# One gate of six with both products in one PSUM bank, on a fused Fourier-mixing and gated-MLP kernel

## The chip, the cores and the metric

The kernel runs on one core of one Trainium2 chip. Five engines work side by side, each through its own instructions in order: TensorE (PE in the profile; its weight loads are PEld), VectorE (DVE), ScalarE (ACT), GpSimd (POOL) and SyncE (SP), which only issues DMA transfers here. The metric is the device time of one execution in microseconds. Before the change three executions took 630.81, 631.33 and 631.26 us, median 631.26 us.

## The reference: what is computed

Input x is 8 batches of 3008 tokens with 256 channels. Both Fourier transforms, over tokens and over channels, are kept as their real part, and the result goes token by token through a gated MLP of width 1536:

```
X = np.fft.fft(x, axis=1)
X = np.fft.fft(X, axis=2)
x = X.real.reshape(8 * 3008, 256)
gate = np.maximum(x @ w_gate, 0.0)
val  = x @ w_val
out  = (gate * val) @ w_out
```

The kernel takes and gives float32; matmuls run on bfloat16 operands.

## The kernel before, in words

**The mirror trick.** The real part of a two-dimensional transform of real data is a sum of a cosine part and a sine part, and the token at the mirrored position has the same cosine part and the sine part with the other sign. So the kernel transforms half the tokens of a batch into two tiles: `U` (cosine, 128 channels by 1505 token columns) and `V` (sine). The channel transform is folded into the weights once: `WA[0]`, `WB[0]` are the gate's weights behind the cosine and sine part, `WA[1]`, `WB[1]` the value's, and `WM = -2 WB` with row 0 zero. A token has gate `a + s` and its mirror `a - s`, with `a = WA·U` and `s = WB·V`.

**Channel 128** has no row of its own among the 128 partitions. Its weights are row 0 of `WB`, and row 0 of `V` carries its values. `b2` holds the gate's channel-128 weights turned upright, one column for each of the 12 groups of 128 hidden units, and `CB` (called `c` in a tile's record) holds channel 128's values on all partitions.

**Tiling.** A batch b ≥ 1 has three blocks of token columns (512, 512 and 481: `thirds`), each with 12 tiles `fi` of 128 hidden units: 36 tiles per batch, 252 in all. Batch 0 has four blocks of 376 or 377 columns (`segments`) and an older form of tile (`first_tile`, `single_tile`).

**A tile of batches 1 to 7** passes through four functions in three successive slots:
- `seed` (L1010): ScalarE writes `c · b2` into a PSUM bank `p`. There are two `p` banks, so it waits until the tile two before has been read out of the same bank.
- `sine_part` (L1015, L1018): TensorE makes `-2s` in bank `g`; ScalarE copies it to a tile `q`. There is one `g` bank.
- `cosine_part` (L1022): TensorE adds `a` into the seeded bank `p`.
- `both` (L1026, L1027): VectorE makes `sp = p - q/2 = a + s`, which frees the bank `p`; GpSimd makes `sm = sp + q = a - s`.
- `value` (L874, L875): TensorE makes the value `a + s` in one of two banks `v`; `relu_mult` (L910) on VectorE multiplies it with `max(sp, 0)`. In the next slot `mirror` (L880) turns the bank `v` into `a - s`, and `second` (L910 again) multiplies it with `max(sm, 0)`.

**A slot** is written out by hand, and nothing reorders it. `slot(cur, mid, nxt, after)` handles four consecutive tiles: `sine_part` of `nxt`; five eighths of the slot's output matmuls (L781, which multiply finished hidden tiles `h` with `wo`); `cosine_part` of `nxt`; `seed` of `after`; `mirror` and `second` of the tile before `cur` (`pending`); `value` and `relu_mult` of `cur`; `both` of `nxt`; one eviction of an output bank on ScalarE, if one is due (L794); the rest of the output matmuls. So the tile `nxt` in the slot of tile `fi` is `fi + 2`. After some slots come three matmuls of the next batch's token transform (`DFT_EVEN`, `DFT_1`: after slots 0, 2, 6 and 8 of the first two blocks), with an eviction (L592, L595) and VectorE sums (L597) behind them. GpSimd folds the input of later batches in between (L198 to L222).

**One exception**: tile 6 of batch 1's first block (`kind` "o") takes the older form, with three matmuls into `g` (`gate`, then `mirror`) and two ScalarE evictions (L890).

**Start of batch 1.** The last tile of batch 0 also starts tiles 0 and 1 of batch 1 (`last`), and the `lead` slot, that of tile 0, follows. In batch 0 every group of output matmuls is followed by `flush`, which issues all due evictions. `gate_128` (L833 to L837) makes `b2` in batch 0's third block with twelve matmuls of one column and a VectorE copy. The weights' own matmuls (`weights`, L427 to L433) are spread over the tiles of batch 0's first block.

Of the kernel before, what the change touches and what calls it, by code (L numbers as in the profile page):

```python
# [29 lines left out]
def dram(ap, offset, pattern):  # L30
    return bass.AP(ap.tensor, offset, [list(p) for p in pattern])
# [3 lines left out]
def kernel(  # L35
# [8 lines left out]
    nc = tc.nc  # L44
    B, S, D = x.shape
    DF = moe_w_gate.shape[1]
    NF = DF // 128
# [3 lines left out]
    NK = NE + NJ  # L51
# [234 lines left out]
    kvec = single("kvec", [128, NK])  # L286
# [133 lines left out]
    def weights(c):  # L420

        f = slice(c * 512, (c + 1) * 512)

        def one(i, T, W):
            p = psO.tile([128, 512], F32, name="o", tag="o")
            for kc in range(2):
                nc.tensor.matmul(p[:], lhsT=T[:, kc, :], rhs=wr[i][c][:, kc, :], start=(kc == 0), stop=(kc == 1))  # L427
            if (i, c, W) == (0, 1, WA):
                return lambda: nc.scalar.copy(W[i][:, f], p[:])
            if (i, W) in ((1, WA), (c - 1, WB)):  # L430
                nc.vector.tensor_scalar(W[i][:, f], p[:], scalar1=1.0, op0=ALU.mult, scalar2=None)  # L431
# [25 lines left out]
    for t in range(3):  # L457
        n = ROWS[1][t]
# [46 lines left out]
    b2 = single("b2", [128, NF])  # L505
    one = single("one", [1, 1], BF16)
    nc.vector.memset(one[:], 1.0)


    def even_table(n, c):  # L510
# [311 lines left out]
    fold_even()  # L822
    turns_and_rows()

    more = {(0, i): [s] for i, s in enumerate(weights(1) + weights(2))}
    for n, c in enumerate(even_order):
        for k, step in enumerate(even_table(n, c)):
            more.setdefault(divmod(EVEN_AT[n] + k, NF), []).append(step)
# [1 line left out]
    for seg in (2, 3):  # L830
        more.setdefault((1, 8 + seg), []).append(lambda seg=seg: minus_v(nc.scalar, seg))

    def gate_128():  # L833
        p = psD.tile([128, 512], F32, name="d", tag="d")
        for f in range(NF):
            nc.tensor.matmul(p[:, f:f + 1], lhsT=WB[0][0:1, f * 128:(f + 1) * 128], rhs=one[:], start=True, stop=True)
        nc.vector.tensor_scalar(b2[:], p[:, 0:NF], scalar1=1.0, op0=ALU.mult, scalar2=None)  # L837
    more[(2, 2)] = [gate_128]
    more_1 = {}
    for at, step in zip((-5, -4, -3, -2, -1, 7, 7, 8, 14, 17), channel_loads() + channel_turn()):  # L840
        (more_1 if at >= 0 else more).setdefault(at if at >= 0 else (3, NF + at), []).append(step)

# [34 lines left out]
    def mirror(bank, st, i):  # L877

        W, v = (WB, st["vm"]) if st["b"] == 0 else (WM, st["vs"])
        nc.tensor.matmul(bank[:, 0:st["n"]], lhsT=W[i][:, st["f"]], rhs=v, start=False, stop=True, skip_group_check=True)  # L880

    def bank(tag):
        return {"g": psG, "p": psP, "v": psV, "d": psD}[tag].tile([128, 512], F32, name=tag, tag=tag)

    def space():
        return rp.tile([128, 512], F32, name="r", tag="r", bufs=12)

    def relu(st):
        st["r"] = space()
        nc.scalar.activation(st["r"][:, 0:st["n"]], st["g"][:, 0:st["n"]], ACTF.Relu)  # L890

    def half_h(st, sign):

        n = st["n"]
        return st["h"][:, 2 * n - 1:n - 1:-1] if sign else st["h"][:, 0:n]

    def mult(st, sign, r=None):
        n = st["n"]
        nc.vector.tensor_tensor(half_h(st, sign), (r or st["r"])[:, 0:n], st["v"][:, 0:n], op=ALU.mult)  # L899

    def keep_rest(st):
        o, h0 = 2 * REST * (st["b"] - 1) % 256, 896
        while h0 < 962:
            k = min(962 - h0, 256 - o)
            nc.sync.dma_start(out=LB[:, st["fi"], o:o + k], in_=st["h"][:, h0:h0 + k])
            o, h0 = 0, h0 + k

    def relu_mult(st, sign):
        n = st["n"]
        nc.vector.scalar_tensor_tensor(half_h(st, sign), in0=st["s"][1 + sign][:, 0:n], scalar=0.0, in1=st["v"][:, 0:n],  # L910
                                       op0=ALU.max, op1=ALU.mult)
# [28 lines left out]
    def single_tile(st, outs, extra=(), last=(), tag="p"):  # L940

        gate(st, tag)
        if pending is not None:
            finish(pending)
        value(st)
        mult(st, 0)
        run(todo_out, outs)
        for step in extra:
            step()
        mirror(st["g"], st, 0)  # L950
        relu(st)
# [52 lines left out]

    def seed(st, p=None):

        if st is None or st["kind"] == "o":
            return
        st["p"] = p or bank("p")
        nc.scalar.activation(st["p"][:, 0:st["n"]], st["c"], ACTF.Copy, scale=b2[:, st["fi"]:st["fi"] + 1])  # L1010

    def sine_part(st):
        n = st["n"]
        st["g"] = bank("g")
        nc.tensor.matmul(st["g"][:, 0:n], lhsT=WM[0][:, st["f"]], rhs=st["vs"], start=True, stop=True)  # L1015
        q = space()
        st["s"] = q, space(), q
        nc.scalar.copy(q[:, 0:n], st["g"][:, 0:n])  # L1018

    def cosine_part(st):  # L1020
        n = st["n"]
        nc.tensor.matmul(st["p"][:, 0:n], lhsT=WA[0][:, st["f"]], rhs=st["us"], start=False, stop=True, skip_group_check=True)  # L1022

    def both(st):
        n, (q, sp, sm) = st["n"], st["s"]
        nc.vector.scalar_tensor_tensor(sp[:, 0:n], in0=q[:, 0:n], scalar=-0.5, in1=st["p"][:, 0:n], op0=ALU.mult, op1=ALU.add)  # L1026
        nc.gpsimd.tensor_tensor(sm[:, 0:n], sp[:, 0:n], q[:, 0:n], op=ALU.add)  # L1027

    def slot(cur, mid, nxt, after, outs, fold_us):
# [5 lines left out]
        old = nxt is not None and nxt["kind"] == "o"  # L1035
        new = nxt is not None and not old
        if old:
            gate(nxt)
        lead = cur["lead"]
        if lead:  # L1040
            out(5)
        if new and mid["kind"] != "o":
            sine_part(nxt)
        out(3 if not lead else 5)
        out(5)
        if new and mid["kind"] == "o":
            sine_part(nxt)
        if new:
            cosine_part(nxt)
        seed(after)  # L1050
        if pending is not None:
            mirror(pending["v"], pending, 1)
        if pending is not None:
            second(pending)
        value(cur)
        if cur["kind"] == "o":
            mult(cur, 0, cur["first"])
        else:
            relu_mult(cur, 0)
        if new:  # L1060
            both(nxt)
        if old:
            nxt["first"] = nxt["r"]
            mirror(nxt["g"], nxt, 0)
            relu(nxt)
        run_fold(fold_us)
        run_one(evict)
        run_one(sums)
        out(8)
        return cur  # L1070
# [142 lines left out]
```

## Time and profile before

| what | value |
|---|---|
| median of three executions | 631.26 us |
| the profiled execution's own time | 630.98 us |
| its span, first to last instruction | 629.2 us |
| PE busy | 620.5 us (99%) |
| DVE busy | 551.5 us (88%) |
| POOL busy | 502.7 us (80%) |
| ACT busy | 445.5 us (71%) |
| granted TensorE clock | 1.00 |

A matmul's row in the timeline gives its start and its length; rows overlap, because matmuls are pipelined, so the step from one start to the next is what a matmul takes of TensorE's time. A row `x5` is five instructions in a run, with the length of the whole run. The brackets at the end of a row give the idle time of its engine just before it, and what ended that. In the groups of instructions the columns are count, busy time, mean length in ns, idle time before them and its releasers.

### The profile page before, as it was taken

The page shows a single profiled execution, that of the slowest core. Times are in us where ns is not written, and L with a number is a line of the kernel's source. Part 1 is how long each engine was busy: PE and PEld are TensorE (multiplying, and loading weights), DVE is VectorE, ACT ScalarE, POOL GpSimd, SP SyncE. Part 2 cuts the span into 40 slices and gives each one's busy share as a digit, 9 for nine tenths or more (in the row PEclk, how much of TensorE's full clock was granted, in tenths as well). Part 3 has the DMA queues.
Part 4 walks back from the last instruction along what each step waited for, and adds up shares of the span by engine and source line. Part 5 has one row for each costly group of instructions (what it writes and reads, how often), then busy time and mean ns, then how long its engine had stood idle before and what let it go on. Part 6 is the DMA issues. An engine that isn't in the chain of part 4 may idle for free.

```text
span 629.2 us, 12441 instructions
## 1 busy us (share of the span) xinstructions
PE 620.5 (99%) x4114; PEld 398.4 (63%) x4114; DVE 551.5 (88%) x981; ACT 445.5 (71%) x813; POOL 502.7 (80%) x478
## 2 busy tenths in 40 slices
PE   8999999999999999999999999999999999999997
PEld 2566666566666666666666666666666666666666
DVE  8886676999899899988999999899999989999991
ACT  7796667777777767777777777777777777777762
POOL 8887992898999988799979989699886566666660
PEclk9999999999999999999999999999999999999999
DMA  9953748734264327315362426211221111211113
GB/s 240 209 206 118 173 177 102 182 73 151 82 150 145 126 76 183 113 44 165 83 187 64 140 76 130 68 50 36 77 61 38 42 60 56 57 38 51 51 44 102
DMA packets 82911, 66.47 MB, mean 106 GB/s; under 512 B 38517, under 2 KB 65941, under 8 KB 82846
## 3 DMA queue, kind: packets, MB, share of 16 engines
q1 hardware_dynamic: 78260, 60.01, 34.3%
q0 software_dynamic: 3984, 4.92, 3.9%
q10 hardware_dynamic: 602, 0.75, 0.4%
q8 instruction: 32, 0.52, 0.4%
q14 instruction: 33, 0.27, 0.2%
HBM read 41.88 MB, written 34.16 MB: 121 GB/s over the span
## 4 chain that ended last, share of the span: by engine, by line
PE 91%; DVE 4%; issue 2%; POOL 1%; DMA 1%; ACT 1%; DVEq 0%; ACTq 0%; POOLq 0%
PE o L781 36%; PE v L880 10%; PE v L875 9%; PE v L874 9%; PE g L1015 8%; PE p L1022 8%; PE d L585 4%; DVE h L910 2%; PE p L880 1%; PE p L874 1%; PE p L875 1%; DMA XG<-in_x_dram,gidx 1%; DVE h L899 1%; DVE r L1026 1%; POOL XG L120 1%
## 5 line engine op out<-in xcount | busy, mean ns | idle before, releaser
L1027 POOL TENSOR_TENSOR r<-r 128x512 f32<-128x512 f32 (+1 forms) x251 | 313.2, 1254 | 100.5 <-DVE r L1026 98.1
L910 DVE SCALAR_TENSOR_TENSOR h<-r,v 128x512 bf16<-128x512 f32 (+1 forms) x502 | 317.1, 673 | 39.2 <-PE v L880 26.5
L781 PE MATMUL o<-wo,h 128*128 128x256 bf16 x2172 | 330.6, 272 | 0.0
L781 PEld LDWEIGHTS <-h 128*128 128x128 bf16 x2220 | 216.7, 98 | 112.0 <-issue 1.3
L1010 ACT ACTIVATE p<-CB,b 128x512 f32<-128x512 bf16 (+1 forms) x251 | 171.8, 684 | 73.4 <-DVE r L1026 72.1
L1018 ACT COPY r<-g 128x512 f32<-128x512 f32 (+1 forms) x251 | 145.1, 578 | 66.5 <-PE g L1015 57.4
L1026 DVE SCALAR_TENSOR_TENSOR r<-r,p 128x512 f32<-128x512 f32 (+1 forms) x251 | 167.9, 669 | 0.9 <-ACT r L1018 0.9
L875 PE MATMUL v<-V,WB 128*128 128x512 bf16 (+3 forms) x296 | 108.6, 367 | 0.0
L874 PE MATMUL v<-U,WA 128*128 128x512 bf16 (+3 forms) x296 | 108.6, 367 | 0.0
L880 PE MATMUL v<-V,WM 128*128 128x512 bf16 (+1 forms) x252 | 94.4, 375 | 0.8 <-DVE h L910 0.4
L1015 PE MATMUL g<-V,WM 128*128 128x512 bf16 (+1 forms) x251 | 94.1, 375 | 0.5 <-ACT r L1018 0.4
L1022 PE MATMUL p<-U,WA 128*128 128x512 bf16 (+1 forms) x251 | 94.1, 375 | 0.2 <-ACT p L1010 0.2
L899 DVE TENSOR_TENSOR h<-r,v 128x376 bf16<-128x376 f32 (+2 forms) x90 | 46.2, 546 | 17.6 <-PE v L880 10.1
L874 PEld LDWEIGHTS <-WA 128*128 128x128 bf16 x348 | 33.9, 97 | 39.5 <-issue 10.4
L875 PEld LDWEIGHTS <-WB 128*128 128x128 bf16 x348 | 34.0, 98 | 34.3 <-DVE WB L431 0.6
L794 ACT COPY os<-o 128x512 f32<-128x512 f32 x92 | 52.6, 571 | 3.5 <-issue 3.0
L198 POOL TENSOR_TENSOR XG<-XG,XD 128x510 f32<-128x510 f32 x42 | 53.0, 1270 | 0.8 <-DMA XG<-xr 0.8
L890 ACT ACTIVATE r<-p 128x376 f32<-128x376 f32 (+1 forms) x80 | 38.0, 486 | 17.8 <-PE p L880 9.0
L206 POOL TENSOR_TENSOR AA<-XG 128x510 f32<-128x510 f32 x42 | 45.5, 1093 | 0.0
L1015 PEld LDWEIGHTS <-WM 128*128 128x128 bf16 x251 | 24.6, 98 | 5.7 <-issue 0.3
L1022 PEld LDWEIGHTS <-WA 128*128 128x128 bf16 x251 | 24.5, 98 | 3.7 <-issue 0.8
L880 PEld LDWEIGHTS <-WM 128*128 128x128 bf16 x253 | 24.8, 98 | 3.1
(186 smaller groups left out, 412.3 us busy)
## 6 DMA issues: line engine op xcount, KB each, us to landing
out_dram<-os SPq DMA_DIRECT2D x124, 128.0 KB
xr<-in_x_dram SPq DMA_DIRECT2D x12, 768.0 KB
XG<-xr SPq DMA_DIRECT2D x12, 768.0 KB
XD<-in_x_dram SPq DMA_DIRECT2D x15, 512.0 KB
out_dram<-os SPq DMA_DIRECT2D x35, 112.0 KB
XD<-in_x_dram SPq DMA_DIRECT2D x8, 448.0 KB
CB<-ch SPq DMA_DIRECT2D x7, 376.2 KB
out_dram<-os SPq DMA_DIRECT2D x13, 96.0 KB
```

The lines of the kernel that those rows point to most:

```text
L198: e.tensor_tensor(XG[p, r, t, ::-1, 1:D], XG[p, r, t, ::-1, 1:D], XD[p, r, t, :, D - 1:0:-1], op=ALU.add)
L781: nc.tensor.matmul(st["p"][0:m, q, :], lhsT=lhs(f), rhs=wo[:, f, :], start=(f == 0 and not (early and q)), stop=(f == NF - 1), skip_group_ ...
L874: nc.tensor.matmul(bank[:, 0:st["n"]], lhsT=WA[i][:, st["f"]], rhs=st["us"], start=True, stop=False)
L875: nc.tensor.matmul(bank[:, 0:st["n"]], lhsT=WB[i][:, st["f"]], rhs=st["vs"], start=False, stop=True)
L880: nc.tensor.matmul(bank[:, 0:st["n"]], lhsT=W[i][:, st["f"]], rhs=v, start=False, stop=True, skip_group_check=True)
L910: nc.vector.scalar_tensor_tensor(half_h(st, sign), in0=st["s"][1 + sign][:, 0:n], scalar=0.0, in1=st["v"][:, 0:n], op0=ALU.max, op1=ALU.mult)
L1010: nc.scalar.activation(st["p"][:, 0:st["n"]], st["c"], ACTF.Copy, scale=b2[:, st["fi"]:st["fi"] + 1])
L1015: nc.tensor.matmul(st["g"][:, 0:n], lhsT=WM[0][:, st["f"]], rhs=st["vs"], start=True, stop=True)
L1018: nc.scalar.copy(q[:, 0:n], st["g"][:, 0:n])
L1022: nc.tensor.matmul(st["p"][:, 0:n], lhsT=WA[0][:, st["f"]], rhs=st["us"], start=False, stop=True, skip_group_check=True)
L1026: nc.vector.scalar_tensor_tensor(sp[:, 0:n], in0=q[:, 0:n], scalar=-0.5, in1=st["p"][:, 0:n], op0=ALU.mult, op1=ALU.add)
L1027: nc.gpsimd.tensor_tensor(sm[:, 0:n], sp[:, 0:n], q[:, 0:n], op=ALU.add)
```

## The change

- Two tiles of every block from batch 1 on, `fi` 2 and 8 (5 and 9 in batch 1's first block), are marked `copied`: 42 of 252. In the slot where such a tile is `nxt`, `cosine_part` comes first, in the place of `sine_part`; `copy_cosine` lets ScalarE write `sm = 2p` from the bank; after `value` of `cur`, `add_sine` adds `WB[0]·V` into the same bank, ScalarE copies it to `sp`, and GpSimd makes `sm = sm - sp`. VectorE's L1026, the bank `g` and the factor `WM[0]` are not used for this tile.
- `WB[0]` row 0 is set to zero on GpSimd after batch 1's second slot, since the seed already carries channel 128.
- Tile 6 of batch 1 is a tile as the others.
- The lead slot has its own order: half of its output matmuls, `sine_part`, `mirror` and `second`, `value` and `relu_mult`, output matmuls, `cosine_part`, `seed`, `both`.
- In `single_tile` the flush comes after `last`.
- The last four steps of `weights` come one tile earlier in batch 0's first block.
- `gate_128` is gone. Row 0 of both `WB` goes to DRAM by two transfers (`keep_128`), comes back spread over partitions by one (`get_128`, 128 x 24 elements of 2 bytes), and ScalarE converts it into a `b2` of 24 columns.
- Three VectorE instructions in batch 0's last block make `WV = -0.5 WM[1]`, 128 x 512 each. What would use it (`short` tiles, `seed_value`, `value_cosine`, `value_sine`, `value_second`) is in the code, but `short` is False for every tile.

```diff
-    more = {(0, i): [s] for i, s in enumerate(weights(1) + weights(2))}
+    more = {(0, i): [s] for i, s in enumerate(weights(1))}
+    for i, step in enumerate(weights(2)):
+        more.setdefault((0, 3 + i), []).append(step)
...
-    def gate_128():
-        p = psD.tile([128, 512], F32, name="d", tag="d")
-        for f in range(NF):
-            nc.tensor.matmul(p[:, f:f + 1], lhsT=WB[0][0:1, f * 128:(f + 1) * 128], rhs=one[:], start=True, stop=True)
-        nc.vector.tensor_scalar(b2[:], p[:, 0:NF], scalar1=1.0, op0=ALU.mult, scalar2=None)
-    more[(2, 2)] = [gate_128]
-    more_1 = {}
+    def keep_128():
+        for i in range(2):
+            nc.sync.dma_start(out=wrow[i:i + 1], in_=WB[i][0:1, :])
+
+    def get_128():
+        nc.sync.dma_start(out=brow[:], in_=dram(wrow, 0, [[1, 128], [128, 2 * NF]]), allow_slow_non_contiguous=True)
+    more[(1, 1)].append(keep_128)
+    more[(1, 4)].append(get_128)
+    more[(2, 2)] = [lambda: nc.scalar.copy(b2[:], brow[:])]
+    for k in range(3):
+        f = slice(512 * k, 512 * k + 512)
+        more[(3, 2 * k + 1)] = [lambda f=f: nc.vector.tensor_scalar(WV[:, f], WM[1][:, f], scalar1=-0.5, op0=ALU.mult, scalar2=None)]
+    more_1 = {1: [lambda: nc.gpsimd.memset(WB[0][0:1, :], 0.0)]}
...
         mirror(st["g"], st, 0)
         relu(st)
-        run(todo_out, outs)
+        for _ in range(outs):
+            run_one(todo_out)
         for step in last:
             step()
+        run(todo_out, 0)
...
-                    st["kind"] = "o" if (b, blk, fi) == (1, 0, 6) else "n"
                     st["lead"] = (b, blk, fi) == (1, 0, 0)
+                    st["copied"] = fi in (2, 8) and (b, blk) != (1, 0) or (b, blk, fi) in ((1, 0, 5), (1, 0, 9))
+                    st["short"] = False
...
+    def copy_cosine(st):
+
+        n, sp, sm = st["n"], space(), space()
+        st["s"] = sm, sp, sm
+        nc.scalar.mul(sm[:, 0:n], st["p"][:, 0:n], 2.0)
+
+    def add_sine(st):
+        n, (_, sp, sm) = st["n"], st["s"]
+        nc.tensor.matmul(st["p"][:, 0:n], lhsT=WB[0][:, st["f"]], rhs=st["vs"], start=False, stop=True, skip_group_check=True)
+        nc.scalar.copy(sp[:, 0:n], st["p"][:, 0:n])
+        nc.gpsimd.tensor_tensor(sm[:, 0:n], sm[:, 0:n], sp[:, 0:n], op=ALU.subtract)
```

The order of a slot after the change:

```python
        if cur["lead"]:
            out(4)
            sine_part(nxt)
            rest_of_pending()
            value_of_cur()
            out(5)
            cosine_part(nxt)
            seed(after)
            both(nxt)
        else:
            if copied:
                cosine_part(nxt)
                copy_cosine(nxt)
            elif nxt is not None:
                sine_part(nxt)
            out(5)
            if nxt is not None and not copied:
                cosine_part(nxt)
            seed(after)
            rest_of_pending()
            value_of_cur()
            if copied:
                add_sine(nxt)
            elif nxt is not None:
                both(nxt)
```

`rest_of_pending` is `mirror` and `second` of the pending tile; `value_of_cur` is `value` and `relu_mult` of `cur`. Eviction and the rest of the output matmuls follow as before.

More of the change, by code (lines that the diff above doesn't have):

```diff
@@ L285 @@
     half_pi = single("half_pi", [128, 1])
-    kvec = single("kvec", [128, NK])
+    kvec = single("kvec", [128, DF // 2])
     dvec = single("dvec", [128, 129], pool=st_)
@@ L504 @@
     ch128 = nc.dram_tensor("ch128", (B, 4 * NJ + 1), BF16, kind="Internal").ap()
-    b2 = single("b2", [128, NF])
-    one = single("one", [1, 1], BF16)
-    nc.vector.memset(one[:], 1.0)
+    wrow = nc.dram_tensor("wrow", (2, DF), BF16, kind="Internal").ap()
+    b2 = single("b2", [128, 2 * NF])
+    brow = single("brow", [128, 2 * NF], BF16)
+    WV = kvec[:].bitcast(BF16)
     def even_table(n, c):
@@ L1005, in seed @@
     def seed(st, p=None):
[L1007 to L1010, printed above, removed]
+        if st is not None:
+            st["p"] = p or bank("p")
+            nc.scalar.activation(st["p"][:, 0:st["n"]], st["c"], ACTF.Copy, scale=b2[:, st["fi"]:st["fi"] + 1])
     def sine_part(st):
@@ L1027, in both, with seed_value, value_cosine, value_sine @@
         nc.gpsimd.tensor_tensor(sm[:, 0:n], sp[:, 0:n], q[:, 0:n], op=ALU.add)
+    def copy_cosine(st):
[7 more added lines that the diff above has]
+        nc.gpsimd.tensor_tensor(sm[:, 0:n], sm[:, 0:n], sp[:, 0:n], op=ALU.subtract)
+    def seed_value(st):
+        st["v"] = bank("v")
+        nc.scalar.activation(st["v"][:, 0:st["n"]], st["c"], ACTF.Copy, scale=b2[:, NF + st["fi"]:NF + st["fi"] + 1])
+    def value_cosine(st):
+        n, st["a"] = st["n"], space()
+        nc.tensor.matmul(st["v"][:, 0:n], lhsT=WA[1][:, st["f"]], rhs=st["us"], start=False, stop=True, skip_group_check=True)
+        nc.scalar.mul(st["a"][:, 0:n], st["v"][:, 0:n], 2.0)
+    def value_sine(st):
+        n = st["n"]
+        nc.tensor.matmul(st["v"][:, 0:n], lhsT=WV[:, st["f"]], rhs=st["vs"], start=False, stop=True, skip_group_check=True)
+    def value_second(st):
+        n = st["n"]
+        a = st["a"][:, 0:n]
+        nc.vector.tensor_tensor(a, a, st["v"][:, 0:n], op=ALU.subtract)
+        nc.gpsimd.tensor_tensor(half_h(st, 1), st["s"][2][:, 0:n], a, op=ALU.mult)
+        if n == 481:
+            keep_rest(st)
     def slot(cur, mid, nxt, after, outs, fold_us):
@@ L1034, in out @@
             run(todo_out, len(todo_out) - stop + outs * part // 8)
[L1035 to L1040, printed above, removed]
-            out(5)
[L1042 to L1048, printed above, removed]
-            cosine_part(nxt)
@@ L1050, in slot, with rest_of_pending @@
[L1050 to L1057, printed above, removed]
-        else:
[L1059 to L1065, printed above, removed]
+        def rest_of_pending():
+            if pending is not None and not pending.get("short"):
+                mirror(pending["v"], pending, 1)
+                second(pending)
@@ new lines, in value_of_cur @@
+        def value_of_cur():
+            if cur["short"]:
+                value_sine(cur)
+            else:
+                value(cur)
+            relu_mult(cur, 0)
+            if cur["short"]:
+                value_second(cur)
+        copied = nxt is not None and nxt["copied"]
+        if cur["short"]:
+            value_cosine(cur)
+        if cur["lead"]:
+            out(4)
+            sine_part(nxt)
+            rest_of_pending()
+            value_of_cur()
+            out(5)
+            cosine_part(nxt)
+            seed(after)
+            both(nxt)
+        else:
+            if copied:
+                cosine_part(nxt)
+                copy_cosine(nxt)
+            elif nxt is not None:
+                sine_part(nxt)
+            out(5)
+            if nxt is not None and not copied:
+                cosine_part(nxt)
+            seed(after)
+            rest_of_pending()
[3 more added lines that the diff above has]
+            elif nxt is not None:
+                both(nxt)
@@ L1066, in slot @@
+        if nxt is not None and nxt["short"]:
+            sm = nxt["s"][2][:, 0:nxt["n"]]
+            nc.gpsimd.tensor_scalar(sm, sm, scalar1=0.0, op0=ALU.max, scalar2=None)
+        if mid is not None and mid["short"]:
+            seed_value(mid)
         run_fold(fold_us)
```

## The prediction

> **What bounds the kernel now.** I read the page's busy times first, then a long stretch of windows, then the groups, then one slot of the timeline row by row.
>
> ```profile
> PE 620.5 (99%) x4114; PEld 398.4 (63%) x4114; DVE 551.5 (88%) x981; ACT 445.5 (71%) x813; POOL 502.7 (80%) x478
> ```
>
> ```profile
> 130.00:600.00 470.00, 469.56 (x3121) 303.99 (x3120) 434.90 (x740) 339.69 (x587) 388.31 (x336) 1.00 0.31 88
> ```
>
> The window's columns are its length, then busy time and count of PE, PEld, DVE, ACT and POOL, the clock, DMA. Batches 1 to 7 are one steady stretch: TensorE is busy 469.56 of 470 us at full clock, VectorE 434.90 (93%). Busy matmuls may still be waiting matmuls, so I look at the steps between their starts. This is the slot of batch 2's last block in which tile 8 is `nxt`, one that the change rewrites:
>
> ```profile
> 240.28 0.67 ACT L1010 ACTIVATE p<-CB,b 128x481 f32<-128x481 bf16 x1 [0.34 <-DVE r L1026]
> ...
> 240.35 1.23 DVE L910 SCALAR_TENSOR_TENSOR h<-r,v 128x481 bf16<-128x481 f32 x2
> ...
> 240.81 0.37 PE L1015 MATMUL g<-V,WM 128*128 128x481 bf16 x1
> ...
> 241.02 0.71 PE L781 MATMUL o<-wo,h 128*128 128x256 bf16 x5
> ...
> 241.27 0.56 ACT L1018 COPY r<-g 128x481 f32<-128x481 f32 x1 [0.32 <-PE g L1015]
> ...
> 241.49 0.65 DVE L1026 SCALAR_TENSOR_TENSOR r<-r,p 128x481 f32<-128x481 f32 x1
> 241.56 0.37 PE L1022 MATMUL p<-U,WA 128*128 128x481 bf16 x1
> ...
> 241.77 0.37 PE L880 MATMUL v<-V,WM 128*128 128x481 bf16 x1
> ...
> 241.97 0.37 PE L874 MATMUL v<-U,WA 128*128 128x481 bf16 x1
> ...
> 242.17 0.67 ACT L1010 ACTIVATE p<-CB,b 128x481 f32<-128x481 bf16 x1 [0.34 <-DVE r L1026]
> 242.17 0.37 PE L875 MATMUL v<-V,WB 128*128 128x481 bf16 x1
> ...
> 242.38 0.49 PE L781 MATMUL o<-wo,h 128*128 128x256 bf16 x3
> ...
> 242.70 0.37 PE L1015 MATMUL g<-V,WM 128*128 128x481 bf16 x1
> ```
>
> A matmul of 481 columns takes a step of 0.20 us (241.56, 241.77, 241.97, 242.17), five of 256 columns take 0.54 (241.02 to 241.56). These steps are the same in all quiet slots, and eight and five of them are the whole slot of 1.89 us: TensorE streams without a hole. VectorE's three instructions, 1.23 and 0.65 us, are 1.88 us of the same 1.89. So TensorE sets the time, and VectorE is just fast enough. Two readings decide about the change:
> - VectorE takes its phase from TensorE: L910 at 242.24 starts when `mirror` (241.77 and 0.37) has ended, then come the second L910 and L1026, and after each round it waits for the next `mirror`.
> - ScalarE's seed L1010 for the next tile waits for L1026 (241.49 and 0.65, end 242.14), starts at 242.17 and ends at 242.84. The next slot starts at 242.70. Likewise the seed from 240.28 ends at 240.95, 0.14 us after this slot's start at 240.81. Today nobody minds: the matmul that needs it, L1022, comes at 241.56.
>
> **The change, part by part.**
>
> *Copied tiles, TensorE.* The count of matmuls is the same, two of the same shape into the gate. But L1022's work moves to the front of the slot, and it needs the seed. In the slot above it could start at 240.95 plus ScalarE's signal to TensorE, not at 240.81. What a signal takes, these rows of batch 1's start show: the seed ends at 105.47 + 0.73 = 106.20, the matmul behind it starts at 106.25, so 0.05 us.
>
> ```profile
> 105.00 0.62 ACT L1018 COPY r<-g 128x512 f32<-128x512 f32 x1
> ...
> 105.47 0.73 ACT L1010 ACTIVATE p<-CB,b 128x512 f32<-128x512 bf16 x1
> ...
> 105.66 0.38 PE L1015 MATMUL g<-V,WM 128*128 128x512 bf16 x1 [0.44 <-ACT r L1018]
> ...
> 106.25 0.38 PE L1022 MATMUL p<-U,WA 128*128 128x512 bf16 x1 [0.21 <-ACT p L1010]
> ```
>
> So this slot begins with a hole of 0.14 + 0.05 = 0.19 us, and everything queued on TensorE waits with it: five output matmuls, `mirror`, `value`. `mirror`, now one matmul earlier in the order, then lands at its old place, and `add_sine` (0.20) lies behind it where nothing lay. The hole can't be made up later, because TensorE has none to spare. With 512 columns there are two more sorts of slot:
>
> ```profile
> 251.68 0.69 ACT L1010 ACTIVATE p<-CB,b 128x512 f32<-128x512 bf16 x1 [0.33 <-DVE r L1026]
> ...
> 252.20 0.38 PE L1015 MATMUL g<-V,WM 128*128 128x512 bf16 x1
> ```
>
> ```profile
> 289.95 0.69 ACT L1010 ACTIVATE p<-CB,b 128x512 f32<-128x512 bf16 x1 [0.36 <-DVE r L1026]
> ...
> 290.10 1.27 DVE L910 SCALAR_TENSOR_TENSOR h<-r,v 128x512 bf16<-128x512 f32 x2
> ...
> 290.38 0.38 PE L1015 MATMUL g<-V,WM 128*128 128x512 bf16 x1
> ...
> 291.14 0.38 PE L1022 MATMUL p<-U,WA 128*128 128x512 bf16 x1
> ...
> 291.42 0.38 PE L880 MATMUL v<-V,WM 128*128 128x512 bf16 x1
> ```
>
> In the first the seed ends at 252.37, hole 0.17 + 0.05 = 0.22 us. In the second, VectorE is late by the sums of the transform: today `mirror` waits until 291.42 for L910 (end 291.37), 0.07 us more than the step of 0.21 (0.20 x 512/481). The seed ends at 290.64, 0.26 after the start, hole 0.31; `mirror` would come at 291.14 + 0.31 = 291.45, 0.03 later than today, and `add_sine`'s 0.22 follows: 0.25 us. I worked out all 42 slots in this way from their own rows: 8 of 0.18 (like 240.81), 6 of 0.20, 12 of 0.22 (like 252.20, or with `mirror` held by VectorE as today), 14 of 0.25 (like 290.38), and none in the 2 of batch 1's first block, whose slots follow three transform matmuls, so that the seed is done. Sum 1.4 + 1.2 + 2.6 + 3.5 = **8.7 us**, on the path.
>
> *Copied tiles, the other engines.* VectorE loses 42 times L1026, 42 x 0.67 = 28 us. It gains nothing by it: after a slot without L1026 it waits for the next `mirror`, as it does after every round. ScalarE gets one more copy of 0.56 to 0.59 us per copied tile (row 241.27). Copied slots are slots 0 and 6 of a block, and there an output eviction is due too (a copy of about the same length): two copies, a seed and an eviction are 2.4 us in a slot of 1.89, but the slot behind has only 1.2. The `sp` copy can start 0.09 us after `add_sine` has ended and runs until about 0.5 us into the slot behind; the eviction and the sine copy of that slot follow, 0.58 each, and end at about 1.7 us, 0.2 us ahead of the next use of bank `g`. I take zero; without that cover it costs up to 0.1 us each, 4 us. `add_sine` needs the doubled copy: cosine end (0.37) plus 0.09 plus 0.58, signal 0.05, about 1.1 us after the cosine's start; ahead of it on TensorE lie 1.2 to 1.4 us. Zero. GpSimd has as many instructions as before, released earlier.
>
> *Batch 1's start and tile 6.* At 105.66 `sine_part` waited for the copy L1018, which had stood behind an eviction; the eviction now follows, so it comes some 0.2 earlier. At 106.25 L1022 waited 0.37 us beyond its step for the seed; it now stands behind three matmuls of `mirror` and `value`. But the eviction delays the next copies. Between 0 and -1.1 I take -0.5. Tile 6:
>
> ```profile
> 113.64 0.38 PE L874 MATMUL g<-U,WA 128*128 128x512 bf16 x1
> ...
> 115.14 0.38 PE L880 MATMUL g<-V,WM 128*128 128x512 bf16 x1
> ...
> 116.20 0.38 PE L1015 MATMUL g<-V,WM 128*128 128x512 bf16 x1
> ```
>
> Its three matmuls become two, -0.22 (the step of 512 columns). The matmul at 116.20 stood behind the second eviction of `g`, which goes. VectorE gets one L1026 more, 0.67. Between 0 and -0.5 I take -0.4.
>
> *Batch 0.*
>
> ```profile
> 30.10 0.32 PE L874 MATMUL d<-U,WA 128*128 128x376 bf16 x1
> ...
> 30.63 0.33 PE L875 MATMUL d<-V,WB 128*128 128x376 bf16 x1 [0.20 <-DVE WB L431]
> ```
>
> ```profile
> 64.29 0.45 PE L836 MATMUL d<-one,WB 1*128 1x1 bf16 x12
> 64.67 0.33 PE L880 MATMUL p<-CB,WB 128*128 128x376 bf16 x1
> ```
>
> The step from 30.10 to 30.63 should be 0.16: the weights came too late by 0.37, and come a tile earlier now: -0.4, at worst 0 if two groups in one tile crowd the banks. `gate_128` takes 0.38 us to the next matmul and 0.1 ahead; what waits on ScalarE behind it appears instead: -0.4, between 0 and -0.5. The new transfers, the `b2` copy and the three `WV` instructions I cost at nothing:
>
> ```profile
> L133 SPq DMA_DIRECT2D CX<-in_x_dram x8: 618/1326/8454, 94.9 to 132.7; - x8
> ```
>
> ```profile
> 41.75 11.20 SPq L806 DMA_DIRECT2D out_dram<-os  x8
> ```
>
> ```profile
> 80.00:120.00 40.00, 39.25 (x261) 25.29 (x260) 29.46 (x57) 27.20 (x54) 25.56 (x24) 1.00 0.70 148
> ```
>
> SP's eight transfers of single elements took 1.3 us each in the middle and 8.5 at most to issue; `get_128` stands between the sixth and the seventh of the eight output transfers that SP has done by 52.95, and ScalarE's copy comes at about 64, 11 us later. Behind it on SP wait those two transfers and the loads of batch 2's input. If it is late, ScalarE's evictions stop behind the copy: up to 3 us. VectorE is busy 29.46 us of 40 around the `WV` instructions; at 0.69 us each (what an instruction of 512 elements takes on this engine above) they are 2.1 us, which its 10.5 idle microseconds hold; uncovered, +2. GpSimd's memset of row 0 lies in a stretch in which it waits for L1026.
>
> *Sum:* 8.7 - 0.5 - 0.4 - 0.4 - 0.4 = +7.0 us. The profiled execution took 630.98 us (span 629.2), so 638.0; the median is 0.28 above it: **638.2 us**.
>
> **Rivals.**
>
> *VectorE was the limit, and is relieved.* `mirror` (L880) waits for VectorE's L910 today where its step from L1022 exceeds 0.21 us:
>
> ```profile
> 110.15 0.38 PE L1022 MATMUL p<-U,WA 128*128 128x512 bf16 x1
> ...
> 110.45 0.38 PE L880 MATMUL v<-V,WM 128*128 128x512 bf16 x1
> ```
>
> ```profile
> 565.87 0.38 PE L1022 MATMUL p<-U,WA 128*128 128x512 bf16 x1
> ...
> 566.31 0.38 PE L880 MATMUL v<-V,WM 128*128 128x512 bf16 x1
> ```
>
> These are the first and the last of 42 such steps, 4.7 us in all over the step itself. Less work on VectorE would end these waits, and the seed would end earlier too, since it follows L1026. From 0.19 to 0.35 us earlier the holes are gone, and 631.3 - 1.7 - 4.7 = **624.9 us**. Against it: the L1026 ahead of the seed belongs to a tile that isn't copied, and its time follows from a `mirror` that doesn't move. Chance 9%. The Trainium skill, page "Perfetto Trace Analysis", section Identifying the Most-Contended Engine, speaks for this rival: matmul busy share is no measure of TensorE's headroom, one goes by occupancy for VectorE and by the weight loads' share for TensorE. By that rule, with 63% and 88% on the page above, VectorE would be the engine to relieve; the trace's steps of 0.20 us don't agree.
>
> *The holes come, but the relief ends other waits.* Half of the 4.7 us lies in slots that aren't copied; if that goes, 638.2 - 2.3 = **635.9**. For it: VectorE is late in those slots. Against: each of its rounds starts anew at a `mirror`. 14%.
>
> *ScalarE becomes late.* The extra copy and the eviction push the sine copy past the next use of `g`: 42 x 0.1, **642.4**. 12%.
>
> *No change:* the holes shrink to what is gained, below 0.05 us each: 2%.
>
> **How the numbers follow.** The forecast has 63%, with 637 to 639.5 as its own range. The range 633.5 to 642.5 takes in the partial relief, a late ScalarE, and terms of batch 0 lost or won. A measurement tells 0.2% (1.3 us) from no change. Faster 0.09, same 0.02, slower 0.89.
>
> **What would show it.** In the changed profile, at the copied slots the cosine matmul, first of its slot, has ScalarE's seed as releaser and starts 0.19 to 0.35 us late, in 40 of 42; VectorE falls by about 26 us and its idle time grows by as much; no waits of `sine_part` for ScalarE in the slots behind. Wrong, if the seeds end before the slots start, or if TensorE's steps elsewhere get shorter than 0.20 and 0.107 us.

## The result and the profile after

The changed kernel takes 646.29 us (median of four executions, 645.73 to 647.27); the kernel before, run beside it, 631.25 us. The ratio is 1.0241, with 1.0224 to 1.0259 as its interval: slower by 15.0 us. The prediction said slower, 638.2 us, and at most 642.5. The direction holds, the time does not: 8 us more than forecast.

Busy times and the groups that answer to those of before, from the page of the changed kernel (L1021 is the seed, L1037 `both`, L919 `relu_mult` and `second`, L1033 the cosine matmul, L1026 the sine matmul; the columns are as before):

```profile
span 644.0 us, 12355 instructions
PE 624.0 (97%) x4056; PEld 399.1 (62%) x4101; DVE 533.5 (83%) x941; ACT 463.5 (72%) x856; POOL 506.2 (79%) x480
...
L919 DVE SCALAR_TENSOR_TENSOR h<-r,v 128x512 bf16<-128x512 f32 (+1 forms) x504 | 318.3, 673 | 71.4 <-PE v L889 54.5
...
L1037 DVE SCALAR_TENSOR_TENSOR r<-r,p 128x512 f32<-128x512 f32 (+1 forms) x210 | 140.5, 669 | 0.6 <-ACT r L1029 0.6
...
L1033 PE MATMUL p<-U,WA 128*128 128x512 bf16 (+1 forms) x252 | 94.4, 375 | 4.4 <-ACT p L1021 2.9
...
L1026 PE MATMUL g<-V,WM 128*128 128x512 bf16 (+1 forms) x210 | 78.8, 375 | 0.1
```

The same groups in the kernel before:

```profile
L910 DVE SCALAR_TENSOR_TENSOR h<-r,v 128x512 bf16<-128x512 f32 (+1 forms) x502 | 317.1, 673 | 39.2 <-PE v L880 26.5 <-PE v L875 1.6 <-POOL r L1027 0.8
...
L1026 DVE SCALAR_TENSOR_TENSOR r<-r,p 128x512 f32<-128x512 f32 (+1 forms) x251 | 167.9, 669 | 0.9 <-ACT r L1018 0.9
...
L1022 PE MATMUL p<-U,WA 128*128 128x512 bf16 (+1 forms) x251 | 94.1, 375 | 0.2 <-ACT p L1010 0.2
```

VectorE has 41 instructions of `both` fewer (42 gone, one more at tile 6), and their time became idle time ahead of L919 (L910 before). Its whole busy time fell by 18.0 us only, not by the 26 forecast; 6.5 us of busy time are the three `WV` instructions, where the prediction had 2.1. New is the idle time ahead of L1033, released by ScalarE's seed. (4056 matmuls against 4101 weight loads: some 45 matmul records are missing, nearly all first ones of `value`, so TensorE's busy time is a little understated.)

Where in the span the 15 us arise is read from one matmul that both traces have, the second one of `value`. For tile 12 of batch 1, the first of its second block, and for the last tile of the kernel, in the timelines of before and of after:

```profile
131.00 0.38 PE L875 MATMUL v<-V,WB 128*128 128x512 bf16 x1
...
615.10 0.37 PE L875 MATMUL v<-V,WB 128*128 128x481 bf16 x1
```

```profile
136.92 0.38 PE L884 MATMUL v<-V,WB 128*128 128x512 bf16 x1
...
630.01 0.37 PE L884 MATMUL v<-V,WB 128*128 128x481 bf16 x1
```

Up to this tile the changed kernel has already lost 5.92 us, where I had forecast a gain of 1.7; behind it, where 40 of the 42 copied tiles lie, it loses 14.91 - 5.92 = 8.99 more, close to the forecast.

The early loss is nearly all in one place of batch 0, around the first of the three `WV` instructions (L847). The timeline of the changed kernel:

```profile
83.36 6.32 POOL L206 TENSOR_TENSOR AA<-XG 128x510 f32<-128x510 f32 x6
...
83.97 5.86 DVE L847 TENSOR_SCALAR kvec<-WM 128x512 bf16<-128x512 bf16 x1
...
86.66 0.32 PE L884 MATMUL p<-V,WB 128*128 128x377 bf16 x1
...
89.64 0.42 POOL L251 TENSOR_TENSOR AA<-XG 128x6 f32<-128x6 f32 x2
...
89.75 0.99 DVE L603 TENSOR_TENSOR U<-es,g 128x376 bf16<-128x376 f32 x2
...
90.67 0.99 DVE L908 TENSOR_TENSOR h<-r,v 128x377 bf16<-128x377 f32 x2
...
91.71 0.46 PE L889 MATMUL v<-CB,WB 128*128 128x377 bf16 x1 [4.73 <-DVE h L908]
...
93.38 0.38 DVE L847 TENSOR_SCALAR kvec<-WM 128x512 bf16<-128x512 bf16 x1
```

An instruction that I priced at 0.69 us took 5.86. It ended at 89.83, 0.15 us after a run of six GpSimd instructions that had begun before it. (GpSimd went on at 89.64 with two short instructions on 6 columns, and these did not hold it longer.) Behind it on VectorE stood L908, which frees a bank that TensorE needs, and TensorE stood for 4.73 us. When TensorE resumed, its clock was half, from 91.76 to 95.18. The windows around it (columns as before; the clock is the last but two):

```profile
88.00:91.70 3.70, 0.00 (x0) 0.00 (x0) 3.66 (x5) 0.00 (x0) 3.62 (x6) 1.00 0.56 132
91.70:94.70 3.00, 2.99 (x12) 1.76 (x12) 1.40 (x3) 0.75 (x2) 1.91 (x2) 0.51 1.03 350
```

The step from 86.66 to 91.71 is 5.05 us where 0.16 was due, +4.89. The matmuls from 91.71 to 95.14 take about twice their usual step, 1.67 us too much in all. Together 6.56 us.

### The profile page after: what moved, and what is told of

The parts are those of the page before. It is cut to its first block, busy times and chain, and to the rows that moved or that the text cites. A ratio compares the mean times of both kernels' runs of the same rounds, so it can differ in the third digit from the quotient of the medians.

```text
span 644.0 us, 12355 instructions
## 1 busy us (share of the span) xinstructions
PE 624.0 (97%) x4056; PEld 399.1 (62%) x4101; DVE 533.5 (83%) x941; ACT 463.5 (72%) x856; POOL 506.2 (79%) x480
## 4 chain that ended last, share of the span: by engine, by line
PE 66%; DVE 18%; issue 6%; ACT 5%; POOL 4%; DMA 1%; SPq 0%; DVEq 0%; ACTq 0%
PE o L782 25%; DVE h L919 10%; PE v L889 7%; PE p L1033 6%; DVE r L1037 6%; PE v L884 6%; PE v L883 5%; PE g L1026 4%; PE d L586 4%; ACT p L1021 4%; POOL r L1038 2%; PE p L1048 1%; PE p L889 1%; PE p L883 1%; PE p L884 1%
## 5 line engine op out<-in xcount | busy, mean ns | idle before, releaser
L919 DVE SCALAR_TENSOR_TENSOR h<-r,v 128x512 bf16<-128x512 f32 (+1 forms) x504 | 318.3, 673 | 71.4 <-PE v L889 54.5
L1021 ACT ACTIVATE p<-CB,b 128x512 f32<-128x512 bf16 (+1 forms) x252 | 172.9, 686 | 57.1 <-DVE r L1037 53.7
L1029 ACT COPY r<-g 128x512 f32<-128x512 f32 (+1 forms) x210 | 121.6, 579 | 52.3 <-PE g L1026 46.7
L1037 DVE SCALAR_TENSOR_TENSOR r<-r,p 128x512 f32<-128x512 f32 (+1 forms) x210 | 140.5, 669 | 0.6 <-ACT r L1029 0.6
L1033 PE MATMUL p<-U,WA 128*128 128x512 bf16 (+1 forms) x252 | 94.4, 375 | 4.4 <-ACT p L1021 2.9
L883 PE MATMUL v<-U,WA 128*128 128x512 bf16 (+3 forms) x254 | 92.9, 366 | 0.0
L1026 PE MATMUL g<-V,WM 128*128 128x512 bf16 (+1 forms) x210 | 78.8, 375 | 0.1
L908 DVE TENSOR_TENSOR h<-r,v 128x376 bf16<-128x376 f32 (+1 forms) x88 | 44.7, 542 | 17.3 <-PE v L889 9.4
L1044 ACT ACTIVATE r<-p 128x512 f32<-128x512 f32 (+1 forms) x42 | 24.8, 589 | 22.0 <-PE p L1033 22.0
L1033 PEld LDWEIGHTS <-WA 128*128 128x128 bf16 x252 | 24.7, 98 | 3.2
```

The costliest lines, as they stand in the source:

```text
L883: nc.tensor.matmul(bank[:, 0:st["n"]], lhsT=WA[i][:, st["f"]], rhs=st["us"], start=True, stop=False)
```

## Experiments

Nothing reads `WV`, so kernels without it compute the same. Each kernel is compared with the kernel before on the same chip (631.05, 631.24 and 631.17 us in the three groups). "Wait" below is what a step between two matmul starts has beyond the same step in a quiet slot (0.21 us for 512 columns, 0.20 for 481, 0.107 for 256), summed over the trace.

### Which part costs what: without WV, WV alone, without WV and copied tiles

```diff
-    for k in range(3):
-        f = slice(512 * k, 512 * k + 512)
-        more[(3, 2 * k + 1)] = [lambda f=f: nc.vector.tensor_scalar(WV[:, f], WM[1][:, f], ...)]
```

> The changed kernel without the three VectorE instructions that make WV, which nothing reads. Theory A (the first of them lost 6 to 7 us: it took 5.86 us beside six GpSimd instructions, TensorE stood for 4.9 us and then ran some 3 us at half clock; the 42 copied tiles cost 9 us): 639.3 us, between 638.6 and 640.0. Rival B (the loss at 84 us only shows a wait that lies elsewhere without the instructions, such as VectorE waiting for GpSimd's WM): above 643 us.

Measured 638.64 us (638.52 to 639.14), ratio 1.0122 [1.0105, 1.0139]. The three instructions cost 646.29 - 638.64 = 7.65 us, and what is left is 0.4 us above the predicted 638.2.

The same three instructions put into the kernel before, with `kvec` widened to hold their result:

> The kernel before with the three WV instructions at the same three places, and nothing else. Theory A: 631.3 + 6.5 to 7.2 = 637.8 to 638.5 us, with one of the three at 5 to 6 us and the other two at 0.4. Rival (the loss needs the changed order of batch 0, through the two transfers of weights or the flush): 631.3 to 633.

Measured 637.18 us, ratio 1.0097 [1.0081, 1.0114]: 6.1 us for them alone. At the place itself 7.65 and 6.1 come closer together. Between a `value` matmul far ahead of it and one behind it (19.70 and 95.80 in the changed kernel) lie 76.10 us with the instructions and 69.58 without, in the kernel before 76.98 and 70.07: they add 6.5 and 6.9 us. What is left of the two totals arises elsewhere in the span, and no run here says why. The timeline of this kernel has the same picture, with about the same time between GpSimd's end (89.78) and VectorE's (89.92):

```profile
83.43 6.35 POOL L206 TENSOR_TENSOR AA<-XG 128x510 f32<-128x510 f32 x6
...
84.15 5.77 DVE L842 TENSOR_SCALAR kvec<-WM 128x512 bf16<-128x512 bf16 x1
```

The changed kernel without `WV` and without copied tiles, so that only the other edits stand:

```diff
-                    st["copied"] = fi in (2, 8) and (b, blk) != (1, 0) or (b, blk, fi) in ((1, 0, 5), (1, 0, 9))
+                    st["copied"] = False
```

> The changed kernel without WV and with no tile copied; the order of batch 1's start, tile 6, the earlier weights and the b2 by transfers stay. Theory A (copied tiles cost 0.18 to 0.25 us each in 40 slots, and one wait of 0.6 us for GpSimd's memset): 639.3 - 9.5 = 629.8 us, at most 630.5, a little faster than before. Rival (the new order of batches 0 and 1 is itself slower, and the copied tiles cost little): 635 us or more.

Measured 630.30 us (ten executions, 630.18 to 630.65), ratio 0.9989 [0.9979, 0.9998]. All other edits together gain 0.75 us (the interval just leaves out no change), and the copied tiles cost 638.64 - 630.30 = 8.34.

### Why WV takes 5.9 us: data, GpSimd or VectorE's queue

First, other data: `WB[1]`, written long before, instead of `WM[1]`.

```diff
-... nc.vector.tensor_scalar(WV[:, f], WM[1][:, f], scalar1=-0.5, ...)
+... nc.vector.tensor_scalar(WV[:, f], WB[1][:, f], scalar1=1.0, ...)
```

> The changed kernel, but the three WV instructions read WB[1], which VectorE and ScalarE wrote long before, and not WM[1], which GpSimd wrote; same engine, shape and type. If the long one waits for a signal of GpSimd's that WM is made, it falls to 0.4 us and the time to about 639.5. If it is held by GpSimd working beside it (the fold, six instructions back to back until 89.7 us), it stays at 5 to 6 us and the time at 646.

Measured 646.05 us in a single execution. The instruction takes as long, so it does not wait for `WM`:

```profile
84.19 5.87 DVE L847 TENSOR_SCALAR kvec<-WB 128x512 bf16<-128x512 bf16 x1
```

Second, the same work on ScalarE at the same places, beside the same GpSimd run:

```diff
-... nc.vector.tensor_scalar(WV[:, f], WM[1][:, f], scalar1=-0.5, ...)
+... nc.scalar.mul(WV[:, f], WM[1][:, f], -0.5)
```

> The changed kernel with the three WV instructions on ScalarE at their old places, beside GpSimd's fold. If only VectorE is held by GpSimd, each takes about 0.6 us and the time is 638.6 to 640 us. If the tiles WM and WV themselves are held (or any engine is slowed beside GpSimd's fold), one takes 5 us and the time is 645 us or more.

Measured 638.55 us in a single execution, as without the instructions at all. The first two of them start at 83.06 and 87.31, beside GpSimd's run, which lasts from 83.13 to 89.46 here. A view of the line gives count, least, median and greatest length in ns:

```profile
L847 ACT ACTIVATE kvec<-WM x3: 632/632/633, 83.1 to 91.5; 128x512 bf16<-128x512 bf16 x3
```

Third, on VectorE but six tiles later, where GpSimd has nothing to do (its next instruction, at 104.79, follows 11.11 us of idle time):

```diff
-        more[(3, 2 * k + 1)] = [...]
+        more.setdefault((3, 2 * k + 7), []).append(...)
```

> The changed kernel with the three WV instructions six tiles later, at tiles 7, 9 and 11 of batch 0's last block, where GpSimd has finished its fold and stands still until batch 1. If GpSimd's work beside it is what held the long one, all three take 0.38 us and the time is that without WV, 638.6 us (638 to 639.5). If the first use of the tile, or the instruction itself, is slow, one takes 5 us again and the time is 643 us or more.

Measured 639.41 us in a single execution:

```profile
L848 DVE TENSOR_SCALAR kvec<-WM x3: 285/285/289, 96.5 to 103.7; 128x512 bf16<-128x512 bf16 x3
```

0.285 us each without GpSimd beside it, 5.86 beside its run of six, and the operand does not matter: the length is GpSimd's. The second `WV` of the changed kernel (93.38, 0.38 us) ended at 93.76, again 0.15 us after a GpSimd instruction that ended at 93.61. The 0.8 us that this one execution is above the kernel without `WV` do not arise at the new place: the same `value` matmul starts 0.33 us later ahead of the three instructions (19.81 against 19.48) and 0.33 us later behind them (105.68 against 105.35). A version with a shorter GpSimd run at the old place wasn't tried.

### Why a copied tile costs 0.2 us: the seed, then VectorE

All kernels of this part are without `WV`. In the first, half of the output matmuls go ahead of the cosine matmul and one behind it, so that the seed is ready:

```diff
             if copied:
+                out(4)
                 cosine_part(nxt)
                 copy_cosine(nxt)
+                out(5)
             elif nxt is not None:
                 sine_part(nxt)
-            out(5)
+                out(5)
+            else:
+                out(5)
```

> No WV; the 42 copied tiles as in the changed kernel, but in their slots half of the output matmuls come ahead of the cosine matmul (0.43 us of cover for the seed) and one behind it, ahead of mirror. Theory A with its second wall: the seed is no longer late, but mirror stands where it stood, one matmul nearer to VectorE's L910 than before the change, and now waits for that: 6.4 us by the same rows (0.07 to 0.22 in a slot) and 0.6 for the memset, 637.3 us (636.5 to 638). Rival (the seed alone makes the hole): 630.9 us.

Measured 637.91 us, ratio 1.0108 [1.0091, 1.0125]: 0.7 us below the order with the cosine first, which the intervals do not separate from no gain, although the wait for the seed is gone. The timeline shows what came in its place:

```profile
279.25 1.28 DVE L916 SCALAR_TENSOR_TENSOR h<-r,v 128x512 bf16<-128x512 f32 x2
...
279.97 0.38 PE L1030 MATMUL p<-U,WA 128*128 128x512 bf16 x1
...
280.18 0.27 PE L782 MATMUL o<-wo,h 128*128 128x256 bf16 x1
...
280.58 0.38 PE L886 MATMUL v<-V,WM 128*128 128x512 bf16 x1
```

`mirror` (L886) was due 0.11 us behind the output matmul at 280.18, but VectorE's second L916 ends at 280.53 and frees its bank only then: 0.29 us. The waits of `mirror` behind an output matmul grew from 2.0 us (without copied tiles) to 10.4. Another 1.6 us come from `add_sine`: in 15 slots it now waits for ScalarE's doubled copy (at 243.70 it starts 0.05 us after that copy has ended).

In the second order two more output matmuls go between cosine and `mirror`, `out(7)` in the place of the inner `out(5)`:

> As the run with the cosine later, but seven eighths of the output matmuls come ahead of mirror, so that mirror stands as late as before the change. Theory A: neither the seed nor VectorE is waited for, 630.3 + 0.6 - 0.1 = 630.8 us (630.2 to 631.5), with 28 us less work on VectorE than before and no gain from it. Rival (VectorE's relief is worth something once the holes are gone): below 629 us. Rival (ScalarE's doubled copy is late for the second matmul): 633 us or more, with that matmul waiting for it.

Measured 629.96 us (ten executions), ratio 0.9981 [0.9972, 0.9991]. Both waits are mostly gone (`mirror`'s behind an output matmul are 3.9 us now); the cost of the 42 copied tiles falls from 8.34 us to -0.34, which the intervals do not separate from nothing. VectorE's relief of 28 us brings no more than that at these places.

In the third the order is that of the change, but the tiles are others, 24 of them, `fi` 5 and 11 of the first two blocks of batches 1 to 6. They are `nxt` in slots 3 and 9, which follow three transform matmuls:

```diff
-                    st["copied"] = fi in (2, 8) and ...
+                    st["copied"] = fi in (5, 11) and blk < 2 and b < B - 1
```

> No WV; copied tiles are fi 5 and 11 in the first two blocks of batches 1 to 6, 24 in all, so that each copied slot (3 and 9) stands behind three transform matmuls. Theory A (a copied slot costs only because ScalarE's seed ends 0.13 to 0.30 us after the slot begins): no holes, since these slots begin 0.47 us later; 630.3 + 0.6 (the wait for the memset) and up to 2.3 less where VectorE's lateness in the slots behind ends: 628.6 to 631.0 us. Rival (a copied tile costs 0.2 us anywhere, by ScalarE's second copy or the second read of the bank): 630.3 + 24 x 0.2 = 635 us.

Measured 627.56 us (627.45 to 627.95), ratio 0.9944 [0.9927, 0.9960], better than I had expected. The timeline of one of its copied slots:

```profile
281.74 0.69 ACT L1018 ACTIVATE p<-CB,b 128x512 f32<-128x512 bf16 x1 [0.37 <-DVE r L1034]
...
282.27 0.65 PE L586 MATMUL d<-tabS,G 128*128 128x377 bf16 x3
282.75 0.38 PE L1030 MATMUL p<-U,WA 128*128 128x512 bf16 x1
```

Without the transform's 0.48 us the cosine matmul would have been due at 282.27, and the seed ends at 282.43; with it there is no hole. And the relief counts here: the waits of `mirror` behind the cosine matmul fall from 5.6 us in 45 steps (without copied tiles) to 2.3 in 15. The slot that the prediction showed at 290.38, without copied tiles and with tiles 5 and 11:

```profile
290.17 0.38 PE L1030 MATMUL p<-U,WA 128*128 128x512 bf16 x1
...
290.47 0.38 PE L886 MATMUL v<-V,WM 128*128 128x512 bf16 x1
```

```profile
289.37 0.38 PE L1030 MATMUL p<-U,WA 128*128 128x512 bf16 x1
...
289.59 0.38 PE L886 MATMUL v<-V,WM 128*128 128x512 bf16 x1
```

A step of 0.30 us has become 0.22. Two further kernels ask whether the place or the relief does it. Tiles 3 and 9 (slots 1 and 7, also behind transform matmuls), 23 of them:

```diff
+                    st["copied"] = fi in (3, 9) and blk < 2 and b < B - 1 and (b, blk, fi) != (1, 0, 3)
```

> No WV; copied tiles are fi 3 and 9 in the first two blocks of batches 1 to 6 (not tile 3 of batch 1's first block), 23 in all, in slots 1 and 7, which also stand behind three transform matmuls. So no hole at the seed either. But VectorE's relief falls into slots 2 and 8, ahead of the next transform matmuls, while mirror waits for VectorE in slots 5, 6, 11 and 12. Theory A (the gain of tiles 5 and 11 is the end of those waits): they stay, 629.5 to 630.6 us. Rival (any copied tile without a hole is worth 0.1 us): 627.6 us as there.

Measured 630.11 us (ten executions), ratio 0.9983 [0.9974, 0.9993], against 630.30 without any, and the two intervals overlap: no holes, but 5.3 us of `mirror`'s waits stay in 42 steps. So it is the place: VectorE must be relieved shortly ahead of the slots in which it is late.

And tiles 5 and 11 without the first of them, which waits for GpSimd's clearing of `WB` row 0:

```diff
+                    st["copied"] = fi in (5, 11) and blk < 2 and b < B - 1 and (b, blk, fi) != (1, 0, 5)
```

> As the run with copied tiles 5 and 11, but tile 5 of batch 1's first block stays as it is, 23 copied tiles: its second matmul waited 0.61 us for GpSimd's memset of the weights. Theory A: 0.6 less for that wait, and about 0.4 more because VectorE's relief is missing there (mirror waits of 0.1 and 0.3 us): 627.4 us (626.8 to 627.9). Rival (that wait was covered by something else): 628.0 us or more.

Measured 626.82 us (626.47 to 626.92), ratio 0.9931 [0.9917, 0.9945]: 4.4 us faster than the kernel before, and the lowest median of all (the interval overlaps that of the 24 tiles).

## Why the prediction was wrong, point by point

**The step that failed** is "the three `WV` instructions I cost at nothing", with the bound "uncovered, +2". They cost 7.65 us between the medians (7.2 between the profiled spans, 644.0 and 636.8; 6.56 of these are the stand and the slow matmuls behind it). I had taken the length of an instruction, 0.69 us, from rows of instructions with an operand in PSUM (this one takes 0.285 us alone), and the cover from a mean, "10.5 idle microseconds" in a window of 40. Both the length and the cover were wrong: the instruction's length was that of GpSimd's run, and the work queued behind it on VectorE was what TensorE waited for next. The trace of before had GpSimd's run at just this place, but no VectorE row of this sort beside such a run, so its price could not be read from it; the bound should have been the length of the run. One hint stood there: VectorE's six instructions L514, of one shape and on tiles in SBUF, took 0.60 to 1.08 us; what stretched the longest no run here shows. This is the run of GpSimd in the timeline of before:

```profile
83.66 6.32 POOL L206 TENSOR_TENSOR AA<-XG 128x510 f32<-128x510 f32 x6
```

The Trainium skill, page "SBUF — State Buffer", section Who interferes with whom, has the rule that I should have weighed: VectorE and GpSimd share a pair of ports, and a `tensor_scalar` of VectorE in one of its two-port modes is blocked fully while an instruction of GpSimd holds it, whereas ScalarE waits for nobody. The trace agrees: 5.86 us beside GpSimd, 0.285 without, 0.63 on ScalarE at the same place. The rule names the one instruction that holds the pair; here VectorE stood through all that were left of six, and why it was not let in between them no run shows.

**Copied tiles**: predicted 8.7 us, measured 8.34. The holes are there, 40 of them as forecast. The slot that answers to the one at 240.81 before:

```profile
248.15 0.67 ACT L1021 ACTIVATE p<-CB,b 128x481 f32<-128x481 bf16 x1 [0.34 <-DVE r L1037]
...
248.35 0.49 PE L782 MATMUL o<-wo,h 128*128 128x256 bf16 x3
248.87 0.36 PE L1033 MATMUL p<-U,WA 128*128 128x481 bf16 x1
```

Due at 248.35 + 3 x 0.11 = 248.68, seed end 248.82, signal 0.05: a hole of 0.19, as predicted. The parts do not agree as well as the sum. The holes are 10.9 us in 40 steps; `mirror`'s waits behind the cosine matmul shrink by 5.6 - 2.5 = 3.1 us, more than the overlap I had counted; and 0.6 us came from a step that I had costed at nothing, GpSimd's memset. 10.9 - 3.1 + 0.6 = 8.4. So a part of the second rival, relief that ends other waits, came true, and the memset hid it. It took 1.37 us for one partition, and the first `add_sine` waited for it:

```profile
117.75 1.37 POOL L848 MEMSET WB<- 1x1536 bf16 x1
...
118.35 0.38 PE L884 MATMUL v<-V,WB 128*128 128x512 bf16 x1
...
119.17 0.39 PE L1048 MATMUL p<-V,WB 128*128 128x512 bf16 x1 [0.45 <-POOL WB L848]
```

0.82 us instead of 0.21. The prediction had put the memset into GpSimd's waiting time. It started right behind an addition of `both` (116.54 to 117.81), and the input of the next one was ready at 118.28: 0.47 us of room for 1.37.

**The gains** were predicted at -1.7 us and measured at -0.75. The earlier weights end the wait at 30.63, but a group of two weight matmuls now waits 0.21 us itself (from 27.98 to 28.35 in the changed kernel); by the starts of `value` in both traces they bring 0.25. The work behind `gate_128` runs ahead by 0.45 us at first, as predicted, and then loses 0.3 of it to `mirror`. The timeline of the kernel with neither `WV` nor copied tiles:

```profile
63.77 0.38 PE L782 MATMUL o<-wo,h 128*128 128x256 bf16 x2
64.01 0.32 PE L886 MATMUL p<-CB,WB 128*128 128x376 bf16 x1
...
66.62 0.32 PE L886 MATMUL v<-CB,WB 128*128 128x376 bf16 x1 [0.29 <-DVE h L905]
```

The start of batch 1 and tile 6 have the rest, by difference about -0.4 us where I had taken -0.9. So it is partly luck that the kernel without `WV` comes within 0.4 us of the forecast: the copied tiles without the memset cost 10.9 - 3.1 = 7.8 us, 0.9 less than predicted, and the memset and the smaller gains put 1.6 us back. That the new transfers cost nothing holds: no wait for them is on TensorE.

**ScalarE late**: not so. `sine_part` (L1026) has 0.1 us of idle time ahead of it in all its 210 instructions, the slots behind the copied ones included. A late ScalarE shows in the order with the cosine later, as `add_sine`'s 1.6 us.

**VectorE relieved**, the rival on the other side: false for the change as it stands, since relief is worth at most some 0.3 us at tiles 2 and 8 even where the new waits are mostly taken away. But it is right at tiles 5 and 11, 627.56 and 626.82 us. My reason against it, that every round of VectorE "starts anew at a `mirror`", holds in quiet slots only; in the slots with transform sums VectorE is behind, and a round saved shortly before is passed on. By the rule of the Trainium skill as the prediction weighed it (page "Perfetto Trace Analysis", section Identifying the Most-Contended Engine), with the weight loads' share for TensorE, VectorE is the engine to relieve: the runs agree for 23 tiles at one place and not for as many at another. The section also names the share of peak matmul work (MFU) for TensorE, which the prediction left out, so the 63% alone do not settle what the rule says here.

## What to carry to other kernels

An instruction "in the idle time" of an engine must be priced by what it could meet there, which is read from the rows of the other engines at its place, and by what is queued behind it, not by the idle share of a window. Where an order is written out by hand, moving a matmul to the front of its slot moves it to the front of its input's arrival: look up when that input ends, and then what waits second once the first wait is gone. Relief of a busy engine is worth something only ahead of the stretch in which others wait for it.

## What the runs showed of the hardware that I had not expected

- A VectorE `tensor_scalar` of 128 x 512 bf16 from SBUF to SBUF took 0.285 us alone and 5.77 to 5.87 us beside a run of six GpSimd instructions on 510 float32 columns. In all six cases, the first and second `WV` instruction of three kernels (changed, before with `WV`, `WB` as operand), it ended some 0.15 us after GpSimd's end. VectorE's L1037 and L919, which read one of their operands from PSUM, keep a mean of 0.67 us though GpSimd is busy 79% of the span.
- After TensorE had stood for 4.7 us the granted clock was 0.50 for 3.4 us (91.76 to 95.18), which cost 1.7 us more than the stand itself. The drop does not go with the end of the stand: with `WB` as operand TensorE resumed at 91.94 at full clock and had half of it from 92.47 to 95.88; with `WV` alone the clock was half from 89.31, within the stand, to 96.13. The Trainium skill, page "TensorE: Matmul & The Clock Gate", section Part 1: The HAM clock gate, gives 3.4 us of idle time as what halves the clock and of work as what restores it; the trace of the changed kernel agrees, with 4.7 us for the one and 3.4 for the other. With `WV` alone it does not: the clock fell 2.15 us after the last matmul had ended (87.16), and TensorE worked 4.33 us, from 91.80, before it was back. There the measurement decides.
- A memset of one partition by 1536 bf16 took 1.37 us on GpSimd, longer than its subtraction of 128 x 512 float32 (1.25 us).
